# Moving the decay products of k from VectorE to GpSimd, and four half sums from DMA to VectorE, in a linear-attention and feed-forward kernel

## The chip, the cores and the metric

The kernel runs on one core of one Trainium2 chip. The metric is the device time of one launch in microseconds, the median of several runs. A profiled execution gives the trace; its span is the time from the first to the last instruction of the core, and a little lies around it.

The engines are called as in the profile: PE (TensorE, matmuls), DVE (VectorE), ACT (ScalarE), POOL (GpSimd) and SP (SyncE, which issues DMAs). Each runs its own instructions in program order; semaphores order the engines among each other.

## The reference

The first half is a recurrence over 768 steps for 4 batches and 8 heads of dimension 48. Its output, with the heads side by side, is a matrix of 3072 tokens by 384. The second half is a feed-forward layer of width 2048 with a rational activation.

```python
f = 1.0 / (1.0 + np.exp(-f_logit))
for t in range(S):
    state = f[:, :, t, :, None] * state + np.einsum('bhd,bhe->bhde', k[:, :, t], v[:, :, t])
    y[:, :, t] = np.einsum('bhd,bhde->bhe', q[:, :, t], state)
...
h = x @ w_in
P = a[0] + a[1] * h + a[2] * h2 + a[3] * h3
Q = 1.0 + np.abs(b[0]) * np.abs(h) + np.abs(b[1]) * h2
g = P / (Q + 1e-06)
return (g @ w_out)
```

## The kernel before

**Units.** The work is cut into 12 units, numbered 0 to 11. A unit is 256 tokens of one batch: unit n has batch n mod 4 and position n div 4 in the sequence. Units 0 to 3 are the starts of the four batches, 4 to 7 their middles, 8 to 11 their ends, so that the state of a batch passes from unit n to unit n + 4. Tokens lie on the 128 partitions, two per partition (index i).

**The order.** The scheduler is off (`tc.manual_schedule()`, line 143). The string ORDER (lines 19 to 97) lists every step of every unit, and the loop at the end calls the steps in that order. Each step puts its instructions at the end of the queue of its engine, so ORDER fixes the order on each engine: a step that is moved in the string is moved past the other steps of its engine, and past the DMA issues of its queue where it issues one. An entry such as `mk 3 0` names the step, the unit and its arguments; `@2` is one of four PSUM slots, which are also taken in this order. A suffix `>name` makes the instruction wait for the named earlier step as well (function `behind`, line 581, and the table `marks`).

**Attention steps of a unit.** `ld` loads f, k, q (SP issues) and v (GpSimd issues). `ef` and `ls` (ScalarE) give the logarithm of the decay; `cs` (PE) sums it over the tokens with triangular matrices; `A` (ScalarE, line 297) takes exp of plus or minus the sum, float32, for k (x = 1) and q (x = 0). `xa` (VectorE, line 303) multiplies q or k with it: `xa n 0` is q's product, `xa n 1` is k's decay product, 768 elements per partition, two float32 inputs in SBUF, into the bfloat16 tile `qkp`; with two more arguments it does a part of the heads. `T` (PE, line 312) transposes both products into PSUM, and `Te` (line 322) copies them to SBUF as `qkT`, on ScalarE where the entry ends in `s`, else on VectorE. `sc` (PE) forms the scores, `mk` (VectorE, line 348) multiplies them, out of PSUM, with a mask. `vm` (GpSimd, line 354) is a small copy of v, 128 elements per partition. `yb` and `yi` (PE) give the output from within the unit and from the state; `kv` and `si` (PE) build the next state in PSUM, `ae` (ScalarE) the decay, and `st` (VectorE, line 442) multiplies the two, reading PSUM. `ye` takes the output to SBUF.

**Feed-forward steps of a unit.** The width of 2048 is 16 blocks of 256 tokens; steps name a range of blocks, so `8 16` is a half of 2048 elements per partition and `0 16` is all 4096. `h` (PE) is the first matmul, `hy` (mostly ScalarE) takes it from PSUM to SBUF in bfloat16. VectorE forms the square (`sq`, line 486) and the absolute value (`ab`, line 494), both out of SBUF. Their sum is made in one of three ways: by PE and identity matmuls (`u`, then `ln` on ScalarE), by an accumulating DMA that GpSimd issues (`zd`, line 516), or on VectorE (`zv`, line 512); after the latter two ScalarE takes the logarithm with `lz`. `ex` (ScalarE) then gives the reciprocal of the denominator. `p1`, `p2` and `pm` (VectorE, lines 528 to 544) build the numerator up to its last addition, which is either an accumulating DMA (`ta`, line 546) or VectorE's `tv` (line 550). `gm` (VectorE, line 554) multiplies numerator and reciprocal, `o` (PE) is the second matmul, `oe` takes its result from PSUM, and `so` stores it (SP or ScalarE issues). `dz` (line 290) are matmuls whose result nobody reads.

**The interleaving.** Steps of several units are in flight at once: while VectorE does the feed-forward products of unit n, the attention of units n + 1 to n + 3 runs. Two tiles `qkp` are used in turn by even and odd units, so the products of unit n + 2 need those of unit n to have been read.

Of the kernel before, what the change touches and what calls it, by code (L numbers as in the profile page):

```python
# [28 lines left out]
yb 1 0 2 @0; vm 2 0; yb 1 2 4; ef 3; st 1 0; sq 0 12 16; p1 0 8 16; yi 1 1; si 1 1; vm 2 1; ye 1 s; h 0 4 8 @1  # L29
h 1 12 16 @0; ls 3; pm 0 8 16; ab 0 12 16; st 1 1; hy 0 4 8; h 1 8 12 @2; sq 0 4 8; hy 1 12 16; hy 1 8 12  # L30
cs 3 @3; p2 0 8 16; ab 0 4 8; h 0 0 4 @0; xa 2 1; h 1 4 8 @2; ab 1 8 16; sq 1 8 16; A 3 1; hy 0 0 4; xa 2 0
u 0 12 16 @0; T 2 @1; hy 1 4 8; A 3 0; ld 3 v; u 0 8 12 @2; sq 0 0 4; ln 0 12 16; Te 2 s; p1 0 0 8; xa 3 1
ab 0 0 4; h 1 0 4 @3; sc 2 0 @0; ln 0 8 12; xa 3 0; p2 0 0 8; hy 1 0 4; kv 2 @1; si 2 0; dz 1 @2; sc 2 1 @3
mk 2 0; ae 2; ld 4 v; st 2 0; mk 2 1; ex 0 8 16; yb 2 0 2 @0; si 2 1; st 2 1; u 0 0 4 @2; ef 5; ln 0 0 4
u 0 4 8 @3; u 1 12 16 @1; ln 0 4 8; yb 2 2 4; yi 2 1; pm 0 0 8; ln 1 12 16; p1 1 0 16; kv 3 @3; wo 8 12; T 3 @2
vm 4 0; ye 2 s; ae 3; ld 4 k; vm 3 0; ef 4; si 3 0; u 1 8 12 @0; h 2 0 4 @1; Te 3 s; sq 1 0 8; ab 1 0 8
pm 1 8 16; st 3 0; ln 1 8 12; ls 4; si 3 1; ld 6 f; ta 0 8 16; ld 5 k; p2 1 0 16; vm 3 1; sc 3 1 @0; wo 12 16
ld 7 f; hy 2 0 4; ex 0 0 8; st 3 1; mk 3 1; h 2 8 12 @2; pm 1 0 8; h 2 4 8 @1; cs 4 @0; sc 3 0 @3; wo 0 4
wo 4 8; hy 2 8 12; A 4 1; A 4 0; h 2 12 16 @2; u 1 4 8 @0; tv 0 0 8; mk 3 0; yb 3 2 4 @3; xa 4 1; ld 5 q; ls 5
hy 2 4 8; hy 2 12 16; yb 3 0 2; yi 3 1; ld 8 f; xa 4 0; cs 5 @1; ye 3 s; T 4 @2; h 3 0 4 @3; gm 0 8 16; ld 6 k  # L40
ln 1 4 8; sq 2 0 16; h 3 12 16 @0; A 5 1; Te 4 s; A 5 0; p1 2 0 16; o 0 1 8 12 @2; hy 3 0 4; u 1 0 4 @1
hy 3 12 16; ef 6; kv 4 @3; o 0 1 12 16; h 3 8 12 @0; ae 4; ln 1 0 4; ld 6 q; ls 6; ab 2 0 16; ld 9 f; ld 7 q
gm 0 0 8; ta 1 8 16; pm 2 0 16; zd 2 8 16; p2 2 0 16; tv 1 0 8; hy 3 8 12; h 3 4 8 @1; ex 1 8 16; sc 4 1 @0
mk 4 1; vm 4 1; ld 5 v; si 4 0; o 0 0 12 16; o 0 1 0 4; o 0 0 0 4; o 0 1 4 8; hy 3 4 8; xa 5 1; st 4 0; ex 1 0 8
ef 7; sc 4 0 @1; mk 4 0; cs 6 @0; o 0 0 8 12; o 0 0 4 8; xa 5 0; yi 4 1 @1; yi 4 0; yb 4 0 2; ld 7 k; A 6 1
yb 4 2 4; oe 0 0 2 s; si 4 1; T 5 @2; A 6 0; ab 3 0 16; sq 3 0 16; ye 4 s; ta 2 0 8; st 4 1; u 2 0 4 @1
h 4 4 8 @0; lz 2 8 16; p1 3 0 16; gm 1 8 16; gm 1 0 8; Te 5 s; h 4 0 4 @3; hy 4 4 8; ln 2 0 4; h 4 12 16 @2
ef 8; h 4 8 12 @0; sc 5 0 @1; pm 3 0 16; hy 4 12 16; zd 3 8 16; hy 4 0 4; u 2 4 8 @2; ta 2 8 16; hy 4 8 12
sc 5 1 @3; mk 5 0; ex 2 8 16; kv 5 @0; ld 6 v; si 5 0; zd 3 0 8; ae 5; vm 5 1; mk 5 1; ld 8 v; o 1 1 12 16 @1
o 1 0 12 16; o 1 0 8 12; ls 7; ln 2 4 8; vm 5 0; sq 4 0 16; st 5 0; xa 6 1; lz 3 8 16; ex 2 0 8; yb 5 0 2 @3  # L50
o 1 1 4 8; xa 6 0; o 1 0 4 8; si 5 1; cs 7 @2; A 7 1; yb 5 2 4; yi 5 0; o 1 1 0 4; yi 5 1; ye 5 s; vm 6 1
ab 4 0 16; p2 3 0 16; o 1 1 8 12; o 1 0 0 4; zd 4 0 8; st 5 1; A 7 0; oe 1 0 2 s; vm 6 0; ta 3 8 16; T 6 @3
# [24 lines left out]
sc 10 1 @2; sc 10 0 @0; h 9 12 16 @3; hy 9 12 16; hy 9 4 8; mk 10 1; ex 7 8 16; mk 10 0; o 6 1 8 12 @2
# [28 lines left out]
def kernel(  # L106
# [12 lines left out]
    nc = tc.nc  # L119
# [18 lines left out]
    ld = ctx.enter_context(tc.tile_pool(name="ld", bufs=3))  # L138
# [173 lines left out]
    def T(n, *args):  # L312
        s = unit(n)
# [311 lines left out]
```

## Time and profile before

| | us |
|---|---|
| median of 3 runs | 218.38 |
| lowest and highest run | 218.06 and 221.5 |
| the profiled execution, its time | 217.21 |
| the profiled execution, its span | 215.4 |

How to read the lines shown below. In the first part of the page stand the busy time of each engine, its share of the span and its number of instructions. A row of the windows has the stretch in us from the span's start, its length, then busy time and number of instructions of PE, PEld (weight loads), DVE, ACT and POOL, then the granted clock of TensorE, the busy share of the DMA engines and GB/s. A row of the timeline has start, duration (of all its instructions, if it merges several: x2), engine, line, operation, output and inputs with their shapes, and in brackets the idle time of the engine ahead of it and who ended it. A row of the groups has line, operation, shapes and count, then total busy time in us and the mean duration in ns, then the idle time before. In shapes, the first number is the partitions and the second the elements on each. Busy time doesn't count DMA issues on SP; a GpSimd row named DMA_DIRECT2D is the issue of a transfer, not the transfer.

### The profile page before, as it was taken

How to read it: one execution, taken by the hardware profiler on the slowest of the kernel's cores; microseconds unless marked ns; L12 is line 12 of the kernel's file. 1: busy time of each engine (PE TensorE's matmuls, PEld its weight loads, DVE VectorE, ACT ScalarE, POOL GpSimd, SP SyncE). 2: the span in 40 equal slices, each digit the busy share in tenths (PEclk: the TensorE clock that was granted, in tenths of full speed). 3: DMA queues.
4: the chain of work that ended last, by engine and by line, in shares of the span. 5: the costliest groups of instructions: out<-in, count | busy, mean ns of one | idle time of the engine just before them, and what ended most of it. 6: DMA issues, size and time to landing. Idle time of an engine off the chain costs nothing.

```text
span 215.4 us, 7124 instructions
## 1 busy us (share of the span) xinstructions
PE 201.7 (94%) x3166; PEld 139.7 (65%) x3166; DVE 202.3 (94%) x213; ACT 195.8 (91%) x204; POOL 79.5 (37%) x93
## 2 busy tenths in 40 slices
PE   5885999899999999999998999999999999999993
PEld 1544687568776685686775677676677676676541
DVE  4787899999999999999999999999999999999981
ACT  3564789999999999999999999999999999999970
POOL 5161008078046084440395352260291403115200
PEclk9999999999999999999999999999999999999999
DMA  5999999986999999999999999699989997976923
GB/s 136 247 256 213 202 233 227 201 165 142 215 209 221 227 209 221 197 266 215 233 253 250 223 185 198 119 239 262 171 156 195 194 200 147 181 227 121 246 88 135
DMA packets 61199, 43.20 MB, mean 201 GB/s; under 512 B 51184, under 2 KB 55024, under 8 KB 61168
## 3 DMA queue, kind: packets, MB, share of 16 engines
q0 software_dynamic: 21520, 23.86, 66.3%
q1 hardware_dynamic: 39360, 18.68, 35.1%
q8 instruction: 25, 0.41, 0.7%
q10 hardware_dynamic: 288, 0.20, 0.3%
q14 instruction: 6, 0.05, 0.1%
HBM read 25.17 MB, written 4.72 MB: 139 GB/s over the span
## 4 chain that ended last, share of the span: by engine, by line
DVE 34%; PE 33%; ACT 11%; DMA 11%; issue 8%; SPq 2%; POOL 1%; DVEq 0%; POOLq 0%
PE hp L453 11%; PE op L566 10%; DVE gall L556 6%; DMA w_in_sb<-in_moe_w_in_dram 6%; DVE h L488 5%; DVE gall L544 5%; DVE scm L352 4%; DVE qkp L307 3%; ACT hy L483 3%; DVE gall L530 3%; DMA fn<-in_f_logit_dram 3%; DVE hy L535 3%; PE y L366 3%; DVE z L496 3%; PE u L504 2%
## 5 line engine op out<-in xcount | busy, mean ns | idle before, releaser
L566 PE MATMUL op<-w_out_sb,gall 128*128 128x384 bf16 x384 | 68.6, 326 | 0.7 <-DVE gall L556 0.5
L453 PE MATMUL hp<-xT,w_in_sb 128*128 128x256 bf16 x564 | 66.6, 273 | 1.9 <-DMA w_in_sb<-in_moe_w_in_dram 1.5
L453 PEld LDWEIGHTS <-w_in_sb 128*128 128x128 bf16 x564 | 54.3, 98 | 12.2 <-DMA w_in_sb<-in_moe_w_in_dram 2.0
L566 PEld LDWEIGHTS <-gall 128*128 128x128 bf16 x384 | 35.7, 98 | 24.3 <-DVE gall L556 1.7
L483 ACT CAST hy<-hp 128x1024 bf16<-128x1024 f32 x47 | 48.6, 1069 | 2.2 <-PE hp L477 1.2
L359 POOL COPY vmp<-vn 128x128 bf16<-128x128 bf16 x24 | 29.3, 1247 | 52.1 <-DMA vn<-in_v_dram 29.3
L526 ACT ACTIVATE qi<-lq 128x2048 bf16<-128x2048 f32 (+1 forms) x26 | 47.4, 1853 | 0.1
L522 ACT ACTIVATE lq<-z 128x2048 f32<-128x2048 bf16 (+1 forms) x20 | 36.4, 1847 | 0.4 <-DMA z<-h 0.4
L518 POOL DMA_DIRECT2D z<-h x17 | 21.4, 1374 | 40.3 <-DMA vn<-in_v_dram 10.9
L352 DVE TENSOR_TENSOR scm<-sc,mask 128x1024 bf16<-128x1024 f32 x24 | 28.9, 1213 | 1.7 <-PE sc L344 1.5
L548 POOL DMA_DIRECT2D gall<-hy x20 | 19.7, 1029 | 26.5 <-ACT hy L483 7.6
L556 DVE TENSOR_TENSOR gall<-gall,qi 128x4096 bf16<-128x4096 bf16 (+2 forms) x17 | 28.1, 1656 | 1.0 <-DMA gall<-hy 0.8
L488 DVE TENSOR_TENSOR h<-hy 128x4096 bf16<-128x4096 bf16 (+2 forms) x19 | 28.4, 1500 | 0.1
L544 DVE TENSOR_TENSOR gall<-gall,h 128x4096 bf16<-128x4096 bf16 (+2 forms) x17 | 28.1, 1652 | 0.0
L301 ACT ACTIVATE A<-cs 128x768 f32<-128x768 f32 (+1 forms) x26 | 20.0, 804 | 2.7 <-PE cs L285 2.5
L535 DVE TENSOR_SCALAR hy<-hy,a_sb 128x4096 bf16<-128x4096 bf16 (+1 forms) x14 | 17.0, 1211 | 0.0
L530 DVE TENSOR_SCALAR gall<-hy,a_sb 128x4096 bf16<-128x4096 bf16 (+1 forms) x14 | 16.9, 1210 | 0.0
L192 POOL DMA_DIRECT2D vn<-in_v_dram x12 | 16.3, 1355 | 0.0
L496 DVE TENSOR_SCALAR z<-hy 128x4096 uint16<-128x4096 uint16 (+2 forms) x19 | 15.9, 839 | 0.0
L329 ACT COPY qkT<-tp 128x1024 f32<-128x1024 f32 x11 | 11.5, 1048 | 3.0 <-PE tp L319 3.0
L270 ACT ACTIVATE fn<-fn 128x768 f32<-128x768 f32 (+1 forms) x13 | 10.8, 830 | 2.8 <-DMA fn<-in_f_logit_dram 2.8
L319 PE MATMUL tp<-ident,qkp 128*128 128x128 bf16 x192 | 12.9, 219 | 0.5 <-DVE qkp L307 0.5
(73 smaller groups left out, 256.3 us busy)
## 6 DMA issues: line engine op xcount, KB each, us to landing
gall<-hy POOLq DMA_DIRECT2D x18, 512.0 KB, 8.1
z<-h POOLq DMA_DIRECT2D x15, 512.0 KB, 8.9
fn<-in_f_logit_dram SPq DMA_DIRECT2D x11, 384.0 KB, 8.7
kn<-in_k_dram SPq DMA_DIRECT2D x11, 384.0 KB, 11.4
qn<-in_q_dram SPq DMA_DIRECT2D x11, 384.0 KB, 10.2
out_dram<-osb SPq DMA_DIRECT2D x11, 384.0 KB, 4.8
vn<-in_v_dram POOLq DMA_DIRECT2D x12, 192.0 KB, 10.5
w_in_sb<-in_moe_w_in_dram POOLq DMA_DIRECT2D x4, 384.0 KB, 9.9
```

The lines of the kernel that those rows point to most:

```text
L352: return nc.vector.tensor_mul(t, s["sc", g].rearrange("s r a i t -> s (r a) (i t)"), mb)
L359: nc.gpsimd.tensor_copy(s["vm"][:, :, :, 32 * x:32 * x + 16], src)
L453: nc.tensor.matmul(t[:, m - m0, :], w_in_sb[:, kk, m * P:(m + 1) * P], s["x"][:, kk].rearrange("p i j t -> p (i j t)"), start=(kk == 0), s ...
L483: (nc.scalar.copy if eng == "s" else nc.vector.tensor_copy)(fl(big(s, "hy", "hy", 3), m0, m1), fl(s["hp", m0], 0, m1 - m0))
L488: return nc.vector.tensor_mul(fl(big(s, "h2", "h2", 2), m0, m1), fl(s["hy"], m0, m1), fl(s["hy"], m0, m1))
L522: nc.scalar.activation(fl(lq, m0, m1), fl(s["z"], m0, m1), AF.Ln, scale=regs[2], bias=1.0 + 1e-6)
L526: nc.scalar.activation(fl(qi, m0, m1), fl(lq, m0, m1), AF.Exp, scale=-1.0)
L530: return nc.vector.tensor_scalar(fl(big(s, "g", "gall", 3), m0, m1), fl(s["hy"], m0, m1), a_sb[:, 3:4], a_sb[:, 2:3], op0=ALU.mult, op1=AL ...
L535: i = (nc.gpsimd if eng == "p" else nc.vector).tensor_scalar(fl(s["hy"], m0, m1), fl(s["hy"], m0, m1), a_sb[:, 1:2], a_sb[:, 0:1], op0=ALU ...
L544: return nc.vector.tensor_mul(fl(s["g"], m0, m1), fl(s["g"], m0, m1), fl(s["h2"], m0, m1))
L556: return nc.vector.tensor_mul(fl(s["g"], m0, m1), fl(s["g"], m0, m1), fl(qi, m0, m1))
L566: nc.tensor.matmul(s["op", j][:, j, 0:DM], s["g"][:, m, P * j:P * j + P], w_out_sb[:, m, :], start=(s["on", j] == 1), stop=(s["on", j] == KF))
```

## The change

1. k's decay products of units 3 and 5 to 11 (`xa n 1`) go from VectorE to GpSimd, each in two pieces (`xg n 1 0 2` and `xg n 1 2 4`, 384 elements per partition). Of unit 4 one half goes to GpSimd and one stays on VectorE. Units 0 to 2 are as before. Each of the 17 pieces waits for a named VectorE step in addition to its data; the VectorE step behind the named one reads PSUM in every case (`mk`, in one case the copy `Te`).
2. Four half sums that were DMAs are VectorE instructions: `zd 2 8 16` and `zd 3 8 16` become `zv`, `ta 1 8 16` and `ta 2 8 16` become `tv`.
3. `Te` of unit 8 is done by VectorE instead of ScalarE.
4. `T` transposes q first and k second (before: k first).
5. Six matmuls of `dz` are gone (the entries `dz 1` of line 33, `dz 2` of line 71 and `dz 3` of line 75); the last `dz 1` uses another PSUM slot.
6. From line 29 of ORDER on the steps stand in a new order, and with it the DMA issues and the PSUM slots. The lines ahead of it (19 to 28) are unchanged.

The pieces with their neighbours on VectorE are these (after `>` the step that a piece waits for, which is VectorE's step ahead of the cover):

```
unit 3   xg 3 1 0 2 >xa.3.0, beside mk 2 0;   xg 3 1 2 4 >mk.2.0, beside mk 2 1, then st 2 0
unit 4   xg 4 1 2 4 >tv.0.0.8, beside mk 3 0, then xa 4 1 0 2
unit 5   xg 5 1 0 2 >pm.2.0.16, beside mk 4 1, then st 4 0;   xg 5 1 2 4 >gm.1.8.16, beside mk 4 0, then xa 5 0
unit 6   xg 6 1 0 2 >pm.3.0.16, beside mk 5 0;   xg 6 1 2 4 >mk.5.0, beside mk 5 1, then st 5 0
unit 7   xg 7 1 0 2 >gm.2.0.16, beside mk 6 1, then pm 4;   xg 7 1 2 4 >p2.4.0.16, beside mk 6 0, then st 6 0
unit 8   xg 8 1 0 2 >sq.5.0.16, beside mk 7 1, then p2 5;   xg 8 1 2 4 >zv.5.8.16, beside mk 7 0, then st 7 0
unit 9   xg 9 1 0 2 >gm.4.0.16, beside Te 8, then p1 6;   xg 9 1 2 4 >st.8.0, beside mk 8 0, then p2 6
unit 10  xg 10 1 0 2 >xa.10.0, beside mk 9 0;   xg 10 1 2 4 >mk.9.0, beside mk 9 1, then pm 7
unit 11  xg 11 1 0 2 >p2.8.0.16, beside mk 10 1;   xg 11 1 2 4 >mk.10.1, beside mk 10 0, then pm 8
```

The diff, with ORDER cut to a few of its lines:

```diff
-yb 1 0 2 @0; vm 2 0; yb 1 2 4; ef 3; st 1 0; sq 0 12 16; p1 0 8 16; yi 1 1; si 1 1; vm 2 1; ye 1 s; h 0 4 8 @1
...
-gm 0 0 8; ta 1 8 16; pm 2 0 16; zd 2 8 16; p2 2 0 16; tv 1 0 8; hy 3 8 12; h 3 4 8 @1; ex 1 8 16; sc 4 1 @0
-mk 4 1; vm 4 1; ld 5 v; si 4 0; o 0 0 12 16; o 0 1 0 4; o 0 0 0 4; o 0 1 4 8; hy 3 4 8; xa 5 1; st 4 0; ex 1 0 8
...
-hy 7 4 8; xa 9 1; Te 8 s; h 7 0 4 @3; hy 7 0 4; st 8 0; sc 8 0 @2; kv 9 @0; p1 6 0 16; ld 10 k; vm 9 0; ta 5 0 8
...
+st 1 0; ab 0 12 16; yb 1 0 2 @0; yb 1 2 4; sq 0 12 16; p1 0 8 16; yi 1 1; si 1 1; ef 3; ye 1 s; h 0 4 8 @2
...
+h 1 0 4 @2; sc 2 0 @1; ln 0 8 12; kv 2 @0; hy 1 0 4; ld 3 v; ld 4 v; xa 3 0; xg 3 1 0 2 >xa.3.0; si 2 0; ae 2
+sc 2 1 @3; mk 2 0; u 0 4 8 @2; u 1 12 16 @1; xg 3 1 2 4 >mk.2.0; mk 2 1; st 2 0; ex 0 8 16; ln 0 4 8; si 2 1
...
+ex 0 0 8; pm 1 0 8; h 2 8 12 @2; h 2 0 4 @1; cs 4 @0; hy 2 0 4; ld 6 f; si 3 1; tv 1 8 16; st 3 1; wo 12 16
...
+o 0 1 12 16; hy 3 12 16; u 1 0 4 @1; hy 3 8 12; ae 4; zv 2 8 16; pm 2 0 16; o 0 1 4 8; si 4 0; o 0 1 8 12
...
+cs 7 @2; A 7 0; yb 5 2 4 @3; yb 5 0 2; zv 3 8 16; sq 4 0 16; ab 4 0 16; A 7 1; yi 5 0; yi 5 1; ye 5 s
+o 1 1 12 16; si 5 1; o 1 0 0 4; st 5 1; kv 6 @2; ld 7 q; o 1 1 4 8; ta 3 0 8; lz 3 8 16; zd 4 0 8; tv 2 8 16
...
+xg 9 1 0 2 >gm.4.0.16; T 8 @0; h 7 0 4 @3; Te 8; si 8 0; ls 10; o 4 0 4 8 @1; p1 6 0 16; sc 8 0 @0; ae 8
...
-    def xa(n, x, *args):
+    def xg(n, x, a0, a1, mark):
+        i = xa(n, x, a0, a1, eng=nc.gpsimd)
+        behind(i, mark[1:])
+        return i
+
+    def xa(n, x, *args, eng=nc.vector):
         s = unit(n)
         a0, a1 = args or (0, HP)
         hh = slice(2 * a0, 2 * a1)
-        return nc.vector.tensor_mul(
+        return eng.tensor_mul(
             s["qk"][:, :, x, hh, 0:D],
...
-        for x in (1, 0):
+        for x in (0, 1):
             for i in range(2):
                 for p in range(a0, a1):
```

129 lines of the change are left out of this document (64 added, 65 removed).

## Prediction, made blind

> **What bounds the kernel now.** I read the page first: busy time by engine, and the chain of waits.
>
> ```profile
> span 215.4 us, 7124 instructions
> PE 201.7 (94%) x3166; PEld 139.7 (65%) x3166; DVE 202.3 (94%) x213; ACT 195.8 (91%) x204; POOL 79.5 (37%) x93
> DVE 34%; PE 33%; ACT 11%; DMA 11%; issue 8%; SPq 2%; POOL 1%; DVEq 0%; POOLq 0%
> ```
>
> Three engines are above 90%, so no share names the bound. The windows, cut at the end of the head (25 us) and at the start of the tail (205 us), do.
>
> ```profile
> 25.00:40.00 15.00, 14.44 (x252) 11.36 (x252) 14.79 (x20) 13.86 (x18) 4.82 (x5) 1.00 1.19 222
> 40.00:95.00 55.00, 54.54 (x947) 38.02 (x947) 55.00 (x50) 55.00 (x62) 26.11 (x25) 1.00 1.11 206
> 95.00:205.00 110.00, 108.08 (x1620) 76.20 (x1618) 109.61 (x90) 109.28 (x101) 39.51 (x40) 1.00 1.00 202
> ```
>
> Columns: length, then busy time of PE, PEld, DVE, ACT, POOL. VectorE is idle for 0.21 + 0 + 0.39 = 0.6 us of these 180, ScalarE for 1.14 + 0 + 0.72 = 1.86 us, PE for 2.9 us. VectorE runs from 25 to 205 us practically without a gap: the time is the head, plus the sum of VectorE's steps, plus the tail. ScalarE is the second bound, hardly looser. GpSimd is busy for 70 of the 180 us and sets nothing. The granted clock is 1.00 throughout. So a VectorE step taken out is worth its full length until ScalarE's 1.86 us are used up, and a step put in costs its full length at once.
>
> **What a step costs.** Consecutive VectorE instructions overlap by some 0.07 us in the records, so I count from start to start.
>
> ```profile
> 8.39 1.02 DVE L307 TENSOR_TENSOR qkp<-kn,A 128x384 bf16<-128x384 f32 x2
> 9.66 0.69 DVE L331 COPY qkT<-tp 128x1024 bf16<-128x1024 bf16 x1 [0.25 <-PE tp L319]
> 10.27 0.55 DVE L307 TENSOR_TENSOR qkp<-qn,A 128x384 bf16<-128x384 f32 x1
> ...
> 66.46 1.21 DVE L552 TENSOR_TENSOR gall<-gall,hy 128x2048 bf16<-128x2048 bf16 x1
> 67.59 1.21 DVE L352 TENSOR_TENSOR scm<-sc,mask 128x1024 bf16<-128x1024 f32 x1
> 68.73 0.94 DVE L307 TENSOR_TENSOR qkp<-kn,A 128x768 bf16<-128x768 f32 x1
> 69.59 0.54 DVE L444 TENSOR_TENSOR state<-sv,alast 128x384 bf16<-128x384 f32 x1
> 70.06 1.21 DVE L352 TENSOR_TENSOR scm<-sc,mask 128x1024 bf16<-128x1024 f32 x1
> 71.19 0.94 DVE L307 TENSOR_TENSOR qkp<-qn,A 128x768 bf16<-128x768 f32 x1
> ```
>
> A half sum (L552; L514 has the same shape) takes 1.13 us of VectorE, a mask product `mk` (L352) 1.14, a whole k product (L307) 0.86 to 0.87, a state product `st` (L444) 0.47. A half k product is (1.02 - 0.07) / 2 = 0.47, and a copy of half of qkT out of PSUM is 10.27 - 9.66 = 0.61.
>
> **Part 1, the k products leave VectorE.** Units 3 and 5 to 11 lose the whole product: 8 x 0.87 = 6.96 us. Unit 4 keeps a half: 0.87 - 0.47 = 0.40. Together -7.36 us.
>
> **Part 2, four half sums come to VectorE.** `tv 1 8 16`, `tv 2 8 16`, `zv 2 8 16` and `zv 3 8 16` replace DMAs: 4 x 1.13 = +4.52 us. The DMAs that go (two `ta`, two `zd`) free GpSimd's queue and the DMA engines, but in the body only ScalarE ever waited for a sum, 0.4 us in all (L522 below), so I count nothing for that, with -0.4 as the most it could give.
>
> **Part 3, one copy changes engine.** In unit 8 `Te` loses its `s`: the copy of qkT goes from ScalarE to VectorE. VectorE's half copy was 0.61, so the whole is at most 2 x 0.61 = 1.22, and if the fixed part is paid once, about the 1.14 of `mk`. I take 1.2, for it is the same operation. ScalarE sheds its copy:
>
> ```profile
> L522 ACT ACTIVATE lq<-z 128x2048 f32<-128x2048 bf16 x17 | 33.0, 1970 | 0.4 <-DMA z<-h 0.4
> ...
> L329 ACT COPY qkT<-tp 128x1024 f32<-128x1024 f32 x11 | 11.5, 1048 | 3.0 <-PE tp L319 3.0
> ```
>
> 1.05 us less an overlap, some 0.97. Sum for VectorE so far: -7.36 + 4.52 + 1.2 = -1.64 us.
>
> **Part 4, what the pieces on GpSimd take back.** There are 17 pieces of 384 elements per partition, each with two float32 inputs in SBUF. No GpSimd row has that form. The nearest:
>
> ```profile
> 0.38 0.10 POOL L609 MEMSET const-bfloat16-1.0<- 128x1 bf16 x1
> ...
> 0.81 0.20 POOL masks.py:65 MEMSET Us<- 128x128 bf16 x1 [0.29 <-POOLq L609]
> ...
> 13.54 0.30 POOL L359 COPY vmp<-vn 128x128 bf16<-128x128 bf16 x1
> ...
> 23.98 0.53 POOL L359 COPY vmp<-vn 128x128 bf16<-128x128 bf16 x2 [6.93 <-DMA vn<-in_v_dram]
> ```
>
> A memset of 1 element takes 0.10 us and of 128 takes 0.20: fixed 0.10, and 0.10 per 128 written. The copy adds one input and 0.10. A second input would add as much again: 0.10 + 3 x (0.10 + 0.10 + 0.10) = 1.0 us; with the copies' spacing in a pair (0.53 - 0.30 = 0.23) for all that is not the second input, 3 x 0.23 = 0.69 is the low end, and twice that, 1.38, the high one. I take 0.9, between the low end and the build-up of 1.0, for a fixed part is counted in each of the three. By the Trainium skill, "GPSIMD Engine Reference", section 3.1, an addition of 2048 float32 elements takes 4497 ns on GpSimd, which prorated is an estimate of 0.84 us for 384; no run here shows it, and the give-back below would be 0.4 us instead of 0.78 by it.
>
> Does a piece cost VectorE anything? The copies of `vm` show that the two engines exclude each other in some steps.
>
> ```profile
> 13.22 1.23 DVE L352 TENSOR_TENSOR scm<-sc,mask 128x1024 bf16<-128x1024 f32 x1
> ...
> 60.73 1.21 DVE L496 TENSOR_SCALAR z<-hy 128x4096 uint16<-128x4096 uint16 x1
> 61.86 1.21 DVE L556 TENSOR_TENSOR gall<-gall,qi 128x2048 bf16<-128x2048 bf16 x1
> 63.00 2.28 DVE L544 TENSOR_TENSOR gall<-gall,h 128x4096 bf16<-128x4096 bf16 x1
> 65.20 1.33 DVE L535 TENSOR_SCALAR hy<-hy,a_sb 128x4096 bf16<-128x4096 bf16 x1
> ...
> 126.51 1.04 DVE L307 TENSOR_TENSOR qkp<-kn,A 128x768 bf16<-128x768 f32 x1
> ```
>
> ```profile
> 62.24 0.86 POOL L518 DMA_DIRECT2D z<-h  x1 [9.23 <-DVE z L496]
> 62.81 2.63 POOL L359 COPY vmp<-vn 128x128 bf16<-128x128 bf16 x1
> ...
> 126.41 0.34 POOL L359 COPY vmp<-vn 128x128 bf16<-128x128 bf16 x1 [3.57 <-DMA vn<-in_v_dram]
> ```
>
> Beside `mk` (13.22) a copy takes its 0.30. Started at 62.81, under products of two SBUF tensors, it takes 2.63 and ends at 65.44, just after the L544 step. The other way round, the copy at 126.41 came first, and the k product after it took 1.04 instead of 0.94. So a piece is free beside `mk`, `st` or the copy from PSUM, and what it hangs over holds the next VectorE step.
>
> The marks put each piece behind a VectorE step whose successor reads PSUM. How late does it start? The `z` issue at 62.24 waited for the L496 step, which ended at 61.94: 0.30 us. The next VectorE step begins 0.07 before that end, so a piece begins 0.37 into it, and a 1.14 us `mk` leaves 0.77 of cover. In ORDER the cover of the pieces is: units 3 and 6, two `mk` and an `st` for both pieces (2.75 us, 2.38 after the start, need 1.8); units 10 and 11, two `mk` (2.28, 1.91 left, need 1.8); the first of unit 5, and the second of 7 and of 8, `mk` and `st` (1.61, 1.24 left, need 0.9); six pieces have one step alone (unit 4, second of 5, first of 7 and 8, both of 9). Only these six hang over, by 0.90 - 0.77 = 0.13: 6 x 0.13 = +0.78 us. At 0.69 us a piece none does: 0. At 1.38 the six cost 6 x 0.61 = 3.7, units 10 and 11 (2.76 - 1.91) x 2 = 1.7, units 3 and 6 (2.76 - 2.38) x 2 = 0.8, and the other three 3 x 0.14 = 0.4: 6.5 us.
>
> On GpSimd's own queue a waiting piece holds back what stands behind it: v loads, `zd`, `ta` and `vm`. In the 55 us from 40 to 95 GpSimd is idle for 28.9, mostly in such waits, and VectorE for none of them: what stands behind them has room. I count 0, bounded by one sum that comes late, the 0.81 us shown for the tail below.
>
> **Part 5, the rest.** Six `dz` filler matmuls go from PE, which has idle time to spare and a granted clock of 1.00 in every window: 0, though what the clock does without them no row shows. In `T`, q is transposed before k: the same 16 transposes, still behind both products for their copy, and PE is not the bound: 0. The new order moves issues on SP too (stores and loads); the loads are issued units ahead: 0. The last wait of VectorE could grow or go:
>
> ```profile
> 205.63 0.69 DVE L556 TENSOR_TENSOR gall<-gall,qi 128x1024 bf16<-128x1024 bf16 x1 [0.81 <-DMA gall<-hy]
> ```
>
> Between -0.81 and +0.81; I take 0.
>
> **Sum.** -1.64 + 0.78 = -0.86 us. The profiled execution took 217.21 us (span 215.4 and 1.8 around it); it would become 216.35. The runs' median, 218.38, lies 1.17 above, so the forecast in their terms is 218.38 - 0.86 = 217.5 us, and 2% of the median, about what a measurement of this kernel can tell from no change, is 4.4 us.
>
> **The rivals.**
> *ScalarE takes over.* The sums come early, the savings late. In 40 to 95 us VectorE gains 4.52 and loses only the products of units 4 (half), 5 and 6, 2.14: +2.4 us, after -0.87 for unit 3. From 95 on it loses five products and gains the copy: -3.15. There ScalarE has 0.72 us idle and sheds 0.97, so that it can follow by 1.69 only. Net +2.4 - 0.87 - 1.69 = -0.16, with the give-back +0.6: 219.0 us. For it: 55.00 of 55.00 us. Against: a new order can let ScalarE work ahead in the first stretch, where VectorE grows.
> *The port decides, slower.* Place: the six pieces with a single step, and the pairs of units 10 and 11. The give-back reaches the 1.64 us saved at about 1.0 us a piece; at 1.38 it is 6.5 us, net +4.9, 223.2 us. For it: the build-up of 1.0 us is at the turning point. Against: that build-up counts a fixed part thrice. A worse form: every piece comes too late for its cover and yet first, and holds a VectorE step of two SBUF tensors for its whole length: 17 x 0.9 = 15.3, net +13.7, 232 us; 0.02 of this case's chance, since the late copy at 62.81 was the one that waited. The rule for it stands in the Trainium skill, "SBUF — State Buffer", section "Who interferes with whom": of a VectorE instruction with two SBUF inputs and a GpSimd instruction that reads SBUF, the one that starts first has the shared port to its end and the other stands still. The trace agrees as far as it goes: the copy at 62.81 stood for 2.3 us.
> *More than the sum.* No piece hangs over, and the tail's wait goes: -1.64 - 0.81 = -2.45, 215.9 us, which ScalarE's idle and its shed copy, 1.86 + 0.97, just allow. For it: every piece has its mark, and 0.69 us is one of the prices. Against: it needs both at once.
> *It doesn't do what it says.* If GpSimd reaches the pieces so late that `T` waits for them, each of 8 units is late by a piece of 0.9 us, of which I would take half as hidden: +3.6, 221.1 us. I count it with the port's chance.
>
> **How the numbers follow.** Forecast 0.45; ScalarE 0.22; the port 0.17; more than the sum 0.16. The likeliest one's own range is 216.7 (no give-back) to 218.4 (all given back). For 8 in 10 I take in ScalarE's case, the third down to where a run lies as far under the median as the profiled one did (215.9 - 1.17 = 214.7), and the port's case up to 1.27 us a piece (six x 0.50, two x 0.63, two x 0.16, three x 0.03, less 1.64: +3.0, 221.4): 214.7 to 221.4. Over 2% faster means under 214.0, beyond the third case's end: 0.06. Over 2% slower means over 222.7, the upper part of the port case: 0.09. Within 2%: 0.85.
>
> **What would show it.** Right: DVE busy without gaps from 25 to 205; pieces on POOL at L315 (the product's line) of 0.8 to 1.0 us that start 0.3 to 0.4 us into an `mk`; the step after a lone `mk` longer by 0.1 to 0.2; no k product on DVE but those of units 0 to 2 and a half; ten sums of 2048 elements on DVE instead of six. The ScalarE rival: gaps on DVE after 95 us ahead of steps that wait for PE or ACT, with ACT full. The port rival: pieces over 1.1 us, and VectorE steps of two SBUF tensors stretched by 0.4 or more. I am wrong if DVE's sum doesn't fall by 1 to 2 us before stretching, or if PE, with those fillers gone, shows a clock under 1.00 in the body.

## The result and the profile after

The changed kernel takes 216.56 us (median of 20 runs, 215.37 to 218.78) against 217.77 us for the kernel before on the same chip (20 runs). The ratio is 0.9947, with an interval of 0.9924 to 0.9971: 1.15 us faster; the interval leaves 1 out, though the gain lies far inside 2%. The experiments ran on three later occasions (e1 to e4, e5 to e8, e9 to e12), each beside the kernel before; the last had the changed kernel itself among them once more: 0.9921 (0.9894 to 0.9948), 1.7 us. Differences of 0.003 between kernels are therefore not told apart below.

The profiled execution of the changed kernel took 217.96 us, more than the one of before (217.21), although its median is lower. From the page of the changed kernel:

```profile
span 216.3 us, 7118 instructions
PE 202.0 (93%) x3152; PEld 139.9 (65%) x3160; DVE 200.9 (93%) x210; ACT 195.0 (90%) x203; POOL 88.6 (41%) x106
PEclk9999699999999999999999999999999999999999
PE 31%; DVE 7%; issue 2%; ACT 1%; ACTq 0%
```

VectorE's busy time fell from 202.3 to 200.9 us, GpSimd's rose from 79.5 to 88.6. The clock row has one slice of 0.6, the fifth of 40, at 21.6 to 27.0 us: this execution lost its extra time in the head, whose order is unchanged. The chain's shares add up to 41% instead of the 100% of before; it was followed back through a part only, so I don't compare it.

To separate head and body, take two VectorE instructions that each kernel has: the state product at the end of the head, and the last product of numerator and reciprocal. First the timeline of VectorE before:

```profile
25.12 0.56 DVE L444 TENSOR_TENSOR state<-sv,alast 128x384 bf16<-128x384 f32 x1 [0.32 <-ACT alast L440]
...
209.62 0.69 DVE L556 TENSOR_TENSOR gall<-gall,qi 128x1024 bf16<-128x1024 bf16 x1
```

then that of the changed kernel (all lines stand 8 lower there):

```profile
27.92 0.56 DVE L452 TENSOR_TENSOR state<-sv,alast 128x384 bf16<-128x384 f32 x1 [1.52 <-ACT alast L448]
...
210.31 0.69 DVE L564 TENSOR_TENSOR gall<-gall,qi 128x1024 bf16<-128x1024 bf16 x1
```

and of the changed kernel's second profile, 216.02 us, the usual time of this kernel:

```profile
26.00 0.56 DVE L452 TENSOR_TENSOR state<-sv,alast 128x384 bf16<-128x384 f32 x1
...
208.36 0.69 DVE L564 TENSOR_TENSOR gall<-gall,qi 128x1024 bf16<-128x1024 bf16 x1
```

From one to the other it is 184.50 us before, and 182.39 and 182.36 after; I call this distance the body below. **The body is 2.1 us shorter**, and the two profiles of the changed kernel agree within 0.03 us. VectorE does the same steps in it in both kernels, but for those that the change moves. What varies is the head: 25.12, 27.92 and 26.00. The windows over just the body, first before, then the changed kernel's second profile:

```profile
25.12:209.62 184.50, 181.07 (x2839) 127.66 (x2839) 183.18 (x164) 181.94 (x182) 70.45 (x70) 1.00 1.03 201
26.00:208.36 182.36, 180.26 (x2832) 127.14 (x2833) 181.75 (x161) 180.47 (x181) 78.71 (x83) 1.00 0.97 189
```

VectorE's busy time (the third) fell by 1.43 us, and its idle time from 1.32 to 0.61. The windows of the changed kernel, first profile, cut as before:

```profile
25.00:40.00 15.00, 14.89 (x222) 11.31 (x222) 13.20 (x20) 13.20 (x17) 3.31 (x5) 0.93 1.11 202
40.00:95.00 55.00, 53.56 (x985) 37.55 (x990) 54.92 (x50) 54.73 (x62) 28.19 (x29) 1.00 1.08 198
95.00:205.00 110.00, 108.80 (x1637) 76.51 (x1636) 109.83 (x88) 109.29 (x101) 48.24 (x52) 1.00 0.95 191
```

VectorE is idle for 0.08 + 0.17 us of the 165 after 40 us; it still sets the time. What moved, from the groups by shape:

```profile
L560 DVE TENSOR_TENSOR gall<-gall,hy 128x2048 bf16<-128x2048 bf16 x6 | 7.2, 1208 | 0.0
L522 DVE TENSOR_TENSOR z<-z,h 128x2048 bf16<-128x2048 bf16 x4 | 4.9, 1233 | 0.0
L315 DVE TENSOR_TENSOR qkp<-kn,A 128x768 bf16<-128x768 f32 x2 | 1.9, 950 | 0.0
L315 DVE TENSOR_TENSOR qkp<-kn,A 128x384 bf16<-128x384 f32 x3 | 1.6, 546 | 0.0
L339 DVE COPY qkT<-tp 128x2048 bf16<-128x2048 bf16 x1 | 1.2, 1210 | 0.0
```

Ten half sums (6 + 4), k products only of units 0 to 2 and half of unit 4, and one whole copy of qkT, recorded with 1.21 us (1.13 from its start to the next step's, where 1.2 was taken). And the pieces, by their line:

```profile
L315 POOL TENSOR_TENSOR qkp<-kn,A x17: 990/1000/1315, 40.8 to 163.8; 128x384 bf16<-128x384 f32 x17
```

The median piece takes **1.00 us**. This is how one lies beside a lone `mk` (unit 8's first). VectorE:

```profile
113.83 1.21 DVE L360 TENSOR_TENSOR scm<-sc,mask 128x1024 bf16<-128x1024 f32 x1
114.96 1.33 DVE L543 TENSOR_SCALAR hy<-hy,a_sb 128x4096 bf16<-128x4096 bf16 x1
```

GpSimd:

```profile
114.05 1.00 POOL L315 TENSOR_TENSOR qkp<-kn,A 128x384 bf16<-128x384 f32 x1 [3.35 <-issue]
```

It begins 0.22 us into the `mk` and ends at 115.05, 0.09 after the next step's start by the records; yet that step, a `p2`, takes 1.33 us as in the quoted row of before. This piece costs nothing. The only piece that costs something is in unit 10. VectorE:

```profile
146.82 2.34 DVE L360 TENSOR_TENSOR scm<-sc,mask 128x1024 bf16<-128x1024 f32 x2
149.09 2.70 DVE L552 TENSOR_TENSOR gall<-gall,h 128x4096 bf16<-128x4096 bf16 x1
```

GpSimd:

```profile
147.10 0.61 POOL L367 COPY vmp<-vn 128x128 bf16<-128x128 bf16 x1
147.35 2.27 POOL L315 TENSOR_TENSOR qkp<-kn,A 128x384 bf16<-128x384 f32 x2
```

Here `vm 10 1` stands ahead of the pair on GpSimd, so the first piece starts 0.53 us into the first `mk`, the pair ends at 149.62, and the `pm` behind the cover takes 2.70 us instead of the 2.28 of the quoted row before: 0.42 us. No other step that a piece hangs over takes longer than its like.

### The profile page after: what moved, and what is told of

It reads as the page before. It is cut to its first block, busy times and chain, and to the rows that moved or that the text cites. A ratio compares the mean times of both kernels' runs of the same rounds, so it can differ in the third digit from the quotient of the medians.

```text
span 216.3 us, 7118 instructions
## 1 busy us (share of the span) xinstructions
PE 202.0 (93%) x3152; PEld 139.9 (65%) x3160; DVE 200.9 (93%) x210; ACT 195.0 (90%) x203; POOL 88.6 (41%) x106
## 5 line engine op out<-in xcount | busy, mean ns | idle before, releaser
L574 PE MATMUL op<-w_out_sb,gall 128*128 128x384 bf16 x384 | 69.6, 326 | 0.7 <-DVE scm L360 0.5
L461 PE MATMUL hp<-xT,w_in_sb 128*128 128x256 bf16 x564 | 67.3, 273 | 3.1 <-DMA w_in_sb<-in_moe_w_in_dram 2.1
L491 ACT CAST hy<-hp 128x1024 bf16<-128x1024 f32 x47 | 48.0, 1060 | 3.1 <-PE hp L485 2.3
L534 ACT ACTIVATE qi<-lq 128x2048 bf16<-128x2048 f32 (+1 forms) x26 | 46.9, 1826 | 0.7 <-DVE gall L564 0.6
L367 POOL COPY vmp<-vn 128x128 bf16<-128x128 bf16 x24 | 21.3, 902 | 26.2 <-DMA vn<-in_v_dram 22.4
L315 POOL TENSOR_TENSOR qkp<-kn,A 128x384 bf16<-128x384 f32 x17 | 17.2, 1035 | 34.4 <-DVE gall L552 11.9
L556 POOL DMA_DIRECT2D gall<-hy x18 | 16.8, 961 | 26.7 <-ACT lq L530 7.6
L526 POOL DMA_DIRECT2D z<-h x15 | 15.4, 1049 | 22.1 <-DVE h L496 7.3
L195 POOL DMA_DIRECT2D vn<-in_v_dram x12 | 14.4, 1199 | 2.6 <-issue 1.5
L337 ACT COPY qkT<-tp 128x1024 f32<-128x1024 f32 x10 | 10.4, 1039 | 3.7 <-PE tp L327 3.5
```

The lines of the kernel that those rows point to most:

```text
L367: nc.gpsimd.tensor_copy(s["vm"][:, :, :, 32 * x:32 * x + 16], src)
L461: nc.tensor.matmul(t[:, m - m0, :], w_in_sb[:, kk, m * P:(m + 1) * P], s["x"][:, kk].rearrange("p i j t -> p (i j t)"), start=(kk == 0), s ...
L491: (nc.scalar.copy if eng == "s" else nc.vector.tensor_copy)(fl(big(s, "hy", "hy", 3), m0, m1), fl(s["hp", m0], 0, m1 - m0))
L534: nc.scalar.activation(fl(qi, m0, m1), fl(lq, m0, m1), AF.Exp, scale=-1.0)
L574: nc.tensor.matmul(s["op", j][:, j, 0:DM], s["g"][:, m, P * j:P * j + P], w_out_sb[:, m, :], start=(s["on", j] == 1), stop=(s["on", j] == KF))
```

## The experiments

All twelve experiments, with the body from one profile of each. Ratios are to the kernel before on the same chip, on the same occasion.

| kernel | median us (runs) | ratio, interval | DVE busy us | body us |
|---|---|---|---|---|
| before | 217.77 (20) | 1 | 202.3 | 184.50 |
| changed | 216.56 (20) | 0.9947, 0.9924 to 0.9971 | 200.9 | 182.39 |
| e1 k back on VectorE | 223.32 (6) | 1.0295, 1.0263 to 1.0327 | 208.1 | 189.61 |
| e2 sums back as DMAs | 229.71 (6) | 1.0571, 1.0545 to 1.0596 | 197.6 | 194.96 |
| e3 no marks | 229.17 (6) | 1.0529, 1.0479 to 1.0579 | 211.7 | 194.94 |
| e4 copy back on ScalarE | 217.06 (12) | 0.9987, 0.9965 to 1.001 | 199.9 | 182.83 |
| e5 fillers in the head | 215.93 (10) | 0.9922, 0.9884 to 0.996 | 201.3 | 183.15 |
| e6 sums as early DMAs | 215.88 (12) | 0.9915, 0.988 to 0.995 | 196.9 | 181.74 |
| e7 sums left out | 215.2 (6) | 0.9864, 0.9808 to 0.992 | 196.9 | 182.41 |
| e8 three `ex` left out | 216.39 (13) | 0.9929, 0.9898 to 0.996 | 200.8 | 182.12 |
| e9 all of the best | 216.1 (6) | 0.9901, 0.9863 to 0.994 | 197.0 | 183.70 |
| e10 before, with fillers | 217.99 (12) | 1.0006, 0.998 to 1.0031 | 202.4 | 184.72 |
| e11 whole k products | 218.31 (12) | 1.0024, 0.9998 to 1.0049 | 202.8 | 184.21 |
| e12 changed, again | 216.37 (11) | 0.9921, 0.9894 to 0.9948 | 200.9 | 182.36 |

**The k products back on VectorE**, all else as changed.

```diff
     def xg(n, x, a0, a1, mark):
-        i = xa(n, x, a0, a1, eng=nc.gpsimd)
-        behind(i, mark[1:])
-        return i
+        return xa(n, x, a0, a1)
```

> The changed kernel with all 17 pieces of k's product on VectorE again, without their marks, in the new order. Theory (VectorE's sum of steps is the time): VectorE gains 16 x 0.47 + 0.47 = 8.0 us in pieces and sheds the 0.43 us by which one step was stretched, so +7.5 us on the changed kernel, about 6.4 us over the kernel before (ratio 1.029). Rival (ScalarE and PE bound it nearly as much, so VectorE's work is partly hidden): +4 us or less on the changed kernel (ratio under 1.013).

The body grew by 189.61 - 182.36 = 7.25 us. By the steps it is 7.36 (part 1), plus 0.07 us for each of the 8 products that stay cut in two, less the 0.42 that a pair gave back: 7.50. The ratio of 1.0295 is the theory's 1.029. The windows from 95 us on show VectorE full and ScalarE (the fourth busy time) with room:

```profile
95.00:205.00 110.00, 105.38 (x1612) 74.38 (x1612) 110.00 (x90) 105.95 (x97) 41.25 (x42) 1.00 0.92 184
```

VectorE sets the time, step for step; a rival in which the move of k is hidden falls.

**The four sums back as DMAs**, at the same places.

```diff
-tv 1 8 16; ... zv 2 8 16; ... zv 3 8 16; ... tv 2 8 16
+ta 1 8 16; ... zd 2 8 16; ... zd 3 8 16; ... ta 2 8 16
```

> The changed kernel with the four half sums as DMAs again, issued by GpSimd at the places of ORDER where VectorE now makes them. Theory with VectorE alone as the bound: -4.5 us (ratio to before 0.974). Rival ScalarE: it is idle for 2.8 us of the 180 in the changed kernel, so at most -2.8 us (ratio 0.982 or more). Rival GpSimd's queue: a sum by DMA lands 6 to 9 us after its issue, and the issues stand behind pieces that wait for their marks, so what uses the sums comes late and nothing is gained or up to 3 us are lost (ratio 0.995 to 1.009).

None of the expectations held: 13.6 us more than the changed kernel, by ratio (1.0571 - 0.9947 = 0.0624 of 217.5), though VectorE has 4.5 us less to do. The windows, cut around the place:

```profile
40.00:95.00 55.00, 52.92 (x938) 37.17 (x927) 52.16 (x46) 50.85 (x58) 30.28 (x34) 1.00 1.14 209
95.00:112.00 17.00, 7.19 (x49) 4.57 (x48) 4.63 (x3) 8.88 (x9) 3.38 (x4) 0.60 0.89 166
112.00:205.00 93.00, 92.47 (x1513) 65.80 (x1512) 92.28 (x69) 92.13 (x86) 40.85 (x44) 1.00 0.90 184
```

VectorE is idle for 2.84 us, then for 12.37 of 17 us. GpSimd's timeline has the issues, VectorE's has the wait:

```profile
90.79 1.26 POOL L526 DMA_DIRECT2D z<-h  x1
92.03 0.90 POOL L556 DMA_DIRECT2D gall<-hy  x1
92.57 2.19 POOL L526 DMA_DIRECT2D z<-h  x1
93.11 2.54 POOL L556 DMA_DIRECT2D gall<-hy  x1
```

```profile
107.37 2.29 DVE L564 TENSOR_TENSOR gall<-gall,qi 128x4096 bf16<-128x4096 bf16 x1 [12.69 <-DMA gall<-hy]
```

Four sums of 512 KB are issued within 5 us, the first and the last of them the ones put back (`zd 3 8 16` and `ta 2 8 16`), and the `gm` of unit 2 needs the last. PE stands too, and its clock in that window is 0.60. Why the transfers took so long isn't settled: from 92 to 108 us the DMA share was 1.05 to 1.29, about the 1.14 of the window ahead. This says that a DMA in the very place of a VectorE sum is no substitute, not that the sums as such are worth 13.6 us; the early DMAs below are the fair comparison.

**No marks**: the pieces stay on GpSimd, and go as soon as their data allow.

```diff
     def xg(n, x, a0, a1, mark):
-        i = xa(n, x, a0, a1, eng=nc.gpsimd)
-        behind(i, mark[1:])
-        return i
+        return xa(n, x, a0, a1, eng=nc.gpsimd)
```

> The changed kernel with the 17 pieces on GpSimd but without their waits on VectorE's steps: a piece begins when its data is there. Theory (the marks put the pieces beside steps out of PSUM, and that is what keeps them free): pieces overlap VectorE steps with two SBUF inputs, pieces of 1.0 us become 2 to 5 us long, several VectorE steps are stretched by 0.3 to 1.0 us, +1 to +6 us on the changed kernel. Rival (GpSimd always loses and waits, so VectorE is not hurt, and the pieces have time): 0 within 0.5 us, pieces long, VectorE steps not stretched.

The body is 194.94 - 182.36 = 12.6 us longer, more than either bound. VectorE has the same 210 instructions, busy for 211.7 us instead of 200.9. Two groups of steps that read SBUF, `p1` and `zv`, in the second profile of the changed kernel:

```profile
L538 DVE TENSOR_SCALAR gall<-hy,a_sb 128x4096 bf16<-128x4096 bf16 x10 | 14.1, 1408 | 0.0
...
L522 DVE TENSOR_TENSOR z<-z,h 128x2048 bf16<-128x2048 bf16 x4 | 4.9, 1233 | 0.0
```

and without marks (lines two lower here):

```profile
L536 DVE TENSOR_SCALAR gall<-hy,a_sb 128x4096 bf16<-128x4096 bf16 x10 | 19.1, 1910 | 0.0
...
L520 DVE TENSOR_TENSOR z<-z,h 128x2048 bf16<-128x2048 bf16 x4 | 7.2, 1799 | 0.0
```

These 14 instructions hold 7.3 of the 10.8 us. One case in the timelines, VectorE and GpSimd:

```profile
66.06 2.14 DVE L536 TENSOR_SCALAR gall<-hy,a_sb 128x4096 bf16<-128x4096 bf16 x1
68.12 2.02 DVE L520 TENSOR_TENSOR z<-z,h 128x2048 bf16<-128x2048 bf16 x1
70.06 2.28 DVE L550 TENSOR_TENSOR gall<-gall,h 128x4096 bf16<-128x4096 bf16 x1
```

```profile
66.11 2.94 POOL L313 TENSOR_TENSOR qkp<-kn,A 128x384 bf16<-128x384 f32 x2 [8.09 <-ACT hy L489]
```

The `p1` took 2.14 instead of 1.33 and the `zv` 2.02 instead of 1.21: 0.81 us each, one piece each, the second of which slipped in between two VectorE steps that followed each other at once. By the Trainium skill, "SBUF — State Buffer", section "Who interferes with whom", whichever of the two engines starts first keeps the shared port to its end. These rows agree only so far: the first piece's record starts 0.05 us behind the `p1`'s, within the 0.07 by which consecutive VectorE records overlap, so they don't tell who was first; and that piece, recorded with 1.00 us, held VectorE for 0.81.

**The copy of unit 8 back on ScalarE.**

```diff
-Te 8;
+Te 8 s;
```

> The changed kernel with unit 8's copy of qkT on ScalarE again; the first piece of unit 9 then has p1 beside it instead of the copy. Theory (VectorE bounds): VectorE sheds 1.14 us, but the piece of unit 9 now stands beside a step out of SBUF and may hold it for up to 1.0 us, so -1.1 to 0 us. Rival (ScalarE bounds): +0.9 us.

VectorE is busy for 1.0 us less, yet the body is 0.47 longer. The ratios differ by 0.004 (against 0.9947) in the direction that the rival expected; their intervals overlap in a strip, so I call it probable. The window from 95 us on shows its mark, VectorE idle for 1.59 us and ScalarE for 0.17:

```profile
95.00:205.00 110.00, 108.61 (x1631) 75.87 (x1630) 108.41 (x88) 109.83 (x101) 46.72 (x51) 1.00 0.93 187
```

The longest two of these waits, 0.50 and 0.46 us, are for ScalarE's decay and for PE's scores. The piece of unit 9 that now has a `p1` beside it is not the reason. VectorE and GpSimd:

```profile
127.46 1.33 DVE L538 TENSOR_SCALAR gall<-hy,a_sb 128x4096 bf16<-128x4096 bf16 x1
```

```profile
127.67 1.98 POOL L315 TENSOR_TENSOR qkp<-kn,A 128x384 bf16<-128x384 f32 x1 [0.53 <-ACT hy L491]
```

It begins 0.21 us into the `p1`, which takes its 1.33 us as ever; it is the piece that stands, 1.98 us in all.

**Fillers in the head**, so that the clock doesn't fall.

```diff
-h 0 8 12 @1; ... ha 0 12 16 @0;
+dz 6 @2; h 0 8 12 @1; ... dz 6 @2; ha 0 12 16 @0;
```

> The changed kernel with twelve filler matmuls more in the head, six ahead of unit 0's first h (blocks 8 to 12) and six ahead of its next (12 to 16), where PE is idle for 1.5 to 2 us each in every trace. In the profiled run of the changed kernel PE's granted clock is 0.5 from 23.6 to 27.0 us, and 12 of its 20 runs have a mean clock of 0.992 or less; these have spans about 1.1 us longer than the others. Theory (PE's idle time in the head lets the clock fall, and that costs about a microsecond): no clock of 0.5 before 40 us, median 0.5 to 1.0 us under the changed kernel's (ratio to before 0.990 to 0.993). Rival (the fall has another cause, or the fillers delay h): same share of runs at 0.992, or 0 to +1 us.

**The kernel before with the same fillers.**

> The kernel before with the same twelve fillers in the head. If the fall of the clock costs about 1.1 us in 17 of 44 runs of the kernel before: no run at a mean clock of 0.992 and a ratio to before of 0.996 to 0.999; the changed kernel with the fillers against this one, both at full clock, is the change alone, expected -1.5 to -2 us (ratio 0.991 to 0.993). Rival (the fillers cost as much as they save): ratio 1.000 or more.

With them no run had a mean clock under 0.997; without, 12 of 20 runs of the changed kernel had 0.992 or less. The head is shorter where the clock holds: the state product begins at 25.20 us in the changed kernel with fillers, at 26.00 and 27.92 without. But the body with fillers is 183.15, 0.79 longer than 182.36, and the times are 0.9922 beside 0.9921, and 1.0006 for the kernel before: no gain that the runs resolve. Why the body lengthens isn't settled; 0.3 us of it is a longer wait for the first `hy` behind the head (0.55 instead of 0.25). With the fillers in both kernels the change is worth 0.9922 / 1.0006 = 0.9916, 1.8 us, as the second expectation had it, though the two ran on different chips.

**The sums as DMAs at the first possible places** (each moved up to right behind the step that makes its input).

```diff
-ta 0 8 16; ... tv 1 8 16;
+ta 0 8 16; ta 1 8 16; ...
-ab 2 0 16; ... zv 2 8 16;
+ab 2 0 16; zd 2 8 16; ...
-sq 3 0 16; ... zv 3 8 16;
+sq 3 0 16; zd 3 8 16; ...
-p2 2 0 16; ... tv 2 8 16
+p2 2 0 16; ta 2 8 16; ...
```

> The changed kernel with the four half sums as DMAs again, each issued by GpSimd at the first place at which its operands are there (units 2 and 3 z sums behind ab and sq, unit 2's numerator behind p2, unit 1's behind the sum of unit 0), so ahead of the pieces. Theory with VectorE alone as the bound: -4.5 us on the changed kernel (ratio to before 0.974). Rival ScalarE, idle 2.8 us in 25 to 205 us: -2.8 us at most (0.982). Rival GpSimd's queue (pieces and sums hold each other up): nothing gained, or slower by up to the 12.7 us stall of the placement tried before.

VectorE sheds 4.0 us of busy time, the body 0.62, the ratio 0.0006 to 0.0032. The theory of VectorE alone (-4.5 us) falls, and the stall of the DMAs before is gone; whether anything was gained at all the runs don't resolve.

**The four sums left out altogether.**

```diff
-tv 1 8 16; ... zv 2 8 16; ... zv 3 8 16; ... tv 2 8 16
```

> The changed kernel with the four half sums left out altogether (the second half of the denominator's sum of units 2 and 3, and of the numerator's last addition of units 1 and 2, are not made), everything else as it is. VectorE does 4.54 us less, no other engine anything else. Theory (VectorE alone sets the time): -4.5 us on the changed kernel, ratio to before 0.974. Rival (ScalarE is the next bound, 2.8 us behind): -2 to -2.8 us, ratio 0.982 to 0.985. Rival (the order as a whole is matched to these times): -1 us or less.

By ratio 1.2 us (against 0.9921) to 1.8 us (against 0.9947) of the 4.5 that VectorE was spared, between the two rivals. The windows say who is next:

```profile
40.00:95.00 55.00, 52.45 (x932) 37.07 (x938) 52.15 (x47) 54.13 (x61) 27.98 (x30) 1.00 1.09 195
95.00:205.00 110.00, 109.42 (x1640) 76.81 (x1639) 109.03 (x88) 109.91 (x103) 46.85 (x51) 1.00 0.94 190
```

VectorE is now idle for 2.85 + 0.97 us and ScalarE for 0.87 + 0.09: by these shares the bound has passed to ScalarE and what feeds it, which no run tests by itself. (The body of this one profile is no shorter; with 216.31 us it is the second slowest of its six runs.)

**Three half reciprocals left out**; ScalarE's busy time falls from 194.9 to 190.3 us.

```diff
-ex 4 0 8; ... ex 6 0 8; ... ex 8 0 8;
```

> The changed kernel with three of ScalarE's steps left out (the reciprocal of blocks 0 to 8 of units 4, 6 and 8), 5.4 us of ScalarE's work in 95 to 180 us, nothing else changed. Theory (VectorE sets the time): within 0.5 us of the changed kernel. Rival (ScalarE is a bound of equal weight): 1 to 2.7 us less.

0.9929 against 0.9947 and 0.9921: nothing. Its profiled execution was its slowest of 13, so I read only the shares:

```profile
95.00:205.00 110.00, 108.94 (x1648) 77.02 (x1647) 110.00 (x88) 104.94 (x99) 48.93 (x54) 1.00 0.95 192
```

ScalarE has 5 us to spare, VectorE none. In the changed kernel ScalarE is not the bound.

**One whole product per unit** instead of two pieces, behind the first mark.

```diff
-xg 8 1 0 2 >sq.5.0.16; ... xg 8 1 2 4 >zv.5.8.16;
+xg 8 1 0 4 >sq.5.0.16; ...
```

(likewise for units 3, 5 to 7 and 9 to 11)

> The changed kernel with each unit's two pieces made one of 768 elements, begun behind the first piece's mark (unit 4's half as it is). Theory (a piece is free while VectorE's steps read PSUM, and what hangs over holds the next step with two SBUF inputs or in a fast mode): a whole piece takes 1.9 us; units 3, 6, 11 have 2.1 us of cover or more: nothing; unit 10 about 0.1, unit 5 about 0.4, units 7, 8 and 9 have one step of cover and hang over by 0.9 us each. Together +3.2 us, less the 0.43 us of today: +2.8 us on the changed kernel, with three VectorE steps (pm of unit 4, p2 of unit 5, p1 of unit 6) stretched by 0.8 to 0.9 us. Rival (VectorE slips in first, GpSimd waits): those steps not stretched, 0 to +0.5 us.

The ratio is 0.0103 above 0.9921, 2.2 us; the body grew by 1.85. Unit 8 again, VectorE and GpSimd:

```profile
114.42 1.21 DVE L360 TENSOR_TENSOR scm<-sc,mask 128x1024 bf16<-128x1024 f32 x1
115.56 1.97 DVE L543 TENSOR_SCALAR hy<-hy,a_sb 128x4096 bf16<-128x4096 bf16 x1
```

```profile
114.64 1.81 POOL L315 TENSOR_TENSOR qkp<-kn,A 128x768 bf16<-128x768 f32 x1 [3.35 <-issue]
```

The product starts at the same 0.22 us into the `mk`, ends 0.89 after the next step's start, and stretches that step by 1.97 - 1.33 = 0.64. Five such stretches, 0.32, 0.77, 0.64, 0.65 and 0.28 for units 5 and 7 to 10, make 2.66, less the 0.42 of the pieces 2.24. The theory's mechanism holds, a little under its 2.8 us; the rival (0 to 0.5) falls. What counts is less than the overhang in the records: 0.25 us less here, 0.12 less behind unit 7's product, which stretches a `pm` by 0.77. VectorE and GpSimd:

```profile
100.23 3.04 DVE L552 TENSOR_TENSOR gall<-gall,h 128x4096 bf16<-128x4096 bf16 x1
```

```profile
99.31 1.81 POOL L315 TENSOR_TENSOR qkp<-kn,A 128x768 bf16<-128x768 f32 x1 [1.90 <-ACT hy L491]
```

Its overhang is the same 0.89. Either way the 0.09 by which a piece of 1.00 us hangs over a lone `mk` is free.

**All of the best together**: the early DMAs, the fillers, and `vm 10 1` moved behind the pair of unit 10.

```diff
-vm 10 1; lz 6 0 8; xg 10 1 0 2 >xa.10.0; ... xg 10 1 2 4 >mk.9.0; mk 9 1;
+lz 6 0 8; xg 10 1 0 2 >xa.10.0; ... xg 10 1 2 4 >mk.9.0; vm 10 1; mk 9 1;
```

> The version that the runs so far point to: the changed kernel with the four half sums as early DMAs, the twelve fillers in the head, and GpSimd's copy vm 10 1 moved behind unit 10's two pieces (ahead of them it made the pieces 0.3 us late, and the second held VectorE's next step for 0.43 us). If the gains add up (0.7, 0.5 and 0.4 us on the changed kernel): ratio to before about 0.987. If ScalarE takes over, as in the kernel with the sums left out: 0.990 to 0.992.

It beats the kernel before (0.9901), but isn't told apart from the changed kernel (0.9921 on the same occasion). The gains didn't add up to the 0.987, and the body of its profile, 183.70, is longer than the changed kernel's. The move of `vm` did half of what it should: the `pm` behind the pair takes 2.47 us there, neither 2.70 nor the 2.28 without a piece.

```profile
148.03 2.47 DVE L552 TENSOR_TENSOR gall<-gall,h 128x4096 bf16<-128x4096 bf16 x1
```

**The changed kernel itself**, on the occasion of e9 to e11.

> The changed kernel as it is, on the same chip as the three others, for a direct comparison: ratio to before 0.995, half of the runs or more at a mean clock of 0.992.

Its 0.9921, lower than the expected 0.995, is the reference for e9 to e11. The runs e1 to e8 had no changed kernel beside them, so they are set against both of its ratios.

## Why the prediction was right, and where not

*What bounds.* Right. Putting the k products back costs their length (7.25 us measured, 7.50 by the steps), and 4.6 us less on ScalarE gives nothing.

*Parts 1 to 3, the sum of -1.64.* Right by the groups: ten half sums, k products where forecast, the copy at 1.13 from start to start instead of 1.2.

*Part 4, the give-back of 0.78 from six lone pieces.* The measured give-back is 0.42, and it comes from elsewhere. Three sizes were off. A piece takes 1.00, not 0.9: the build-up of 1.0 was exact, and the discount for counting a fixed part thrice was wrong. It starts 0.22 us into the step, not 0.37: the lag was taken from a DMA issue, and a product starts sooner. And VectorE waits 0.12 to 0.25 us less than the records overlap. The prediction's own rows had a hint of that: the copy at 126.41 runs 0.24 us into the product at 126.51, which took only 0.10 longer. With 1.00 us and the lag of 0.37 the working would have given 6 x 0.23 + 2 x 0.09 = 1.56, which would have eaten nearly all of the saving; the other two sizes turned that into nothing. That the first error didn't show in the time is luck, and the sign that was named for it, a step 0.1 to 0.2 us longer behind a lone `mk`, didn't come. By the estimate of 0.84 us, prorated from the 4497 ns in the Trainium skill, "GPSIMD Engine Reference", section 3.1, pieces would be still cheaper; the measurement is 1.00.

*GpSimd's queue, counted as 0.* Wrong in one place, and it is the whole give-back: the step "what stands behind them has room" looked behind the pieces, and the loss comes from a copy ahead of one, in a pair that was counted free.

*DMAs that go, counted as 0.* The same sums as well-placed DMAs make the body 0.62 us shorter. So VectorE's 4.52 us for them cost the time about 0.6 us and no more, where the sum by steps charged all of it, since the next bound stands so close that 4.5 us less on VectorE can't be cashed. Sum and result agree nevertheless, for the kernel that was forecast has the sums on VectorE, and there VectorE is the bound.

*The tail.* Taken as 0, within -0.81 to +0.81. The wait of 0.81 us is gone: VectorE's longest wait after 200 us is now the 0.10 ahead of its last product (208.36 less the end of the step ahead, 208.26), which was there before too. Why it went, with the tail's order changed as well, no run separates. So the body should have shrunk by 1.64 - 0.42 + 0.81 = 2.0; it shrank by 2.1. The third rival, more than the sum, thus has the better half of its mechanism in the body; the head gave part of it back.

*The forecast in microseconds.* 217.5 against 216.56. Of these 0.9, 0.6 are the reference: the median of three runs before was 218.38, that of twenty 217.77. The change itself was -0.86 forecast and -1.15 (-1.65 to -0.63) and -1.7 measured. That the first two lie so close is in part luck: for the body the sum was 1.2 us short (0.36 too much give-back, and the tail's 0.81), and the head took about as much back in the runs in which the clock fell.

*The rivals.* ScalarE doesn't take over in this kernel, but by the shares it is the next bound, 1 to 2 us behind (the sums left out, the copy put back). The port is real: unmarked pieces cost 12.6 us, whole products 2.2. The marks keep it away. The forecast's argument against the worse form, that the late engine waits, was too kind: GpSimd doesn't always lose between two VectorE steps.

*The clock.* I named a clock under 1.00 in the body as a sign of being wrong. There is a window of 0.93, but its cause is one dip in the head, ahead of where the first removed `dz` stood (38.76 us in the trace of before), and the kernel before has runs with the same mean clock of 0.992 too. It isn't the fillers' removal. The fall has a price, though. Over all runs of these two kernels whose clock is on record, the changed kernel's span is 213.8 us (median of 12) where the mean clock was 0.997 or more and 215.0 (19) where it was lower; for the kernel before it is 215.9 (36) and 216.1 (35). So the change is worth 2.1 us where the clock holds, just what the body says, and 1.1 where it fell. Why the fall costs the changed kernel more isn't shown.

## What to carry to other kernels

An elementwise product can leave a full VectorE for GpSimd if each piece is tied to the start of a VectorE step that reads PSUM and is short enough for that cover; cut the pieces to the cover and look at what stands ahead of them on GpSimd as well as behind. Take the start lag from an instruction of the same kind, and measure the held time by the stretch of the next step, not by the overlap in the records. When the bound and the next one are 1 to 2 us apart, a saving on one engine is worth that much and no more, and the place of a DMA can count for more than the engine time that it saves (here 14 us between two places of the same four sums, which save VectorE 4.5).

## What the runs showed of the hardware

- A product of two float32 inputs in SBUF with bfloat16 output takes 1.00 us on GpSimd for 384 elements per partition and 1.81 for 768, against 0.54 and 0.94 on VectorE.
- A piece that is recorded with 1.00 us holds a VectorE step that reads SBUF for 0.81 us; a product of 1.81 us whose record overhangs by 0.89 holds a `p2` (one SBUF tensor) for 0.64 and a `pm` (two) for 0.77.
- GpSimd gets in between two VectorE steps that follow each other at once (at 68 us without marks), though other copies stand for over 2 us; a piece that came 0.21 us into a `p1` stood until that ended, 1.98 us in all.
- After four accumulating DMAs of 512 KB had been issued within 5 us, the step that needed the last of them waited 12.69 us; the DMA share until then was 1.05 to 1.29, against 1.14 ahead of it.
